# An explicit order for the first loads, and six planner numbers, in a packed-attention and ELU feed-forward kernel

## The chip, the core and the metric

The kernel runs on one core of a Trainium2 chip. The metric is the device time of one launch in microseconds. The core's engines are named as in the profile: PE (TensorE, matrix products; PEld is its weight load), DVE (VectorE), ACT (ScalarE), POOL (GpSimd) and SP (SyncE, which only issues the DMAs that are looked at here).

## What is computed

```python
def sm_attn(qq, kk, vv):                      # softmax attention, scale 1/sqrt(64)
    s = scale * np.matmul(qq, kk.transpose(0, 1, 3, 2))
    a = softmax(s)
    return np.matmul(a, vv)
p_packed = sm_attn(p, k, v)                   # p: (8, 8, 32, 64); q, k, v: (8, 8, 576, 64)
out      = sm_attn(q, p_packed, p_packed)
x = out.transpose(0, 2, 1, 3).reshape(4608, 512)
h = x @ w_in                                  # (512, 2048)
g = np.where(h > 0, h, np.exp(np.minimum(h, 0)) - 1)
result = g @ w_out                            # (2048, 512)
```

The attention inputs are 32-bit floats. The two weight matrices are given as 64-bit floats.

## The kernel before

**Work and tiles.** There are eight batches (b0 to b7) of 576 tokens. For each batch the kernel does the packed attention: scores of the 32 packed rows against the keys (`s1`, L476), softmax, transposes (`tr1`, L531), product with the values (`pv`, L557), a transpose (L583), then scores of the queries (`s2`, L602, in two halves) and their softmax, which ends in an "unfold" (a DVE transpose, L652) that gives the attention weights `a`. Instead of forming the attention output, it forms M = p_packed times w_in in four column pieces (`mstep`, L705), and h = a times M for sixteen feature blocks f of 128 (`mm`, L815 or L822, called the h steps here). ELU runs on ACT (L829, L835) and DVE (L838), and the output product (`out_mm`, L932 to L941) accumulates over f in PSUM.

**Weights.** Each of the 16 blocks of w_in (named i0 to i15 here) and of w_out (o0 to o15) arrives as a 512 KB tile `raw` of 64-bit words. Seven instructions turn it into 32-bit values: exponent (DVE, L280), sign (ACT, L292), power (ACT, L287), mantissa (DVE, L295), whole (DVE, L301), signed (DVE, L308) and product (DVE, L318). `whole` is the last reader of the raw tile. There are three raw buffers (L237), so a fourth raw load waits until the first tile has been read. For products that use split operands a value is cut in a high part (ACT, L252) and a low part (DVE, L331). The first four w_out blocks are used whole at first and are split later, with due times `T_WS + f` (L351, L352). The weights `a` of batches 0 and 1 are likewise used whole at first, and split at their first use plus `T_AS` (L679).

**The planner.** Every step of the kernel is an entry of a list with a due time, the engines that it may run on with a cost each, the entries that it depends on, and the buffers that it takes. `schedule` (L155) walks through planned time: whenever an engine is free, it takes the entry of earliest due time that is ready and has its buffers, and never interrupts a step. The instructions are then issued in that order, and each engine and the SP queue work strictly through their own list. The due times are counted in h steps: h step number i is due at i, its output product at i + `LOOK`. The conversion of a weight block is due `LI` or `LO` ahead of its first use, and an M piece of batches 0 and 1 `LM` ahead of it. The attention of b0 is due at -40 to -36, and its second `s2` half at `T_S2`. Batch 1 follows `T_ATT1`. Later batches follow `T_ATT` and `TM`.

**Modes of PE.** Entries on PE carry a mode: 1 for products with 64-row operands (s1, s2, mstep), 2 for pv, none for the rest. When the next entry would change the mode, the planner looks for a ready entry of the present mode whose due time is less than `STAY` later than that entry's (L183), and takes it instead.

**The first loads.** The loads of i0 to i3 are due at -60 to -57 and those of o0 and o1 at about -44 (L335). The loads of b0 are due at -46 (packed rows p and keys k), -45 (values v, in two parts) and -43 (queries q). All of these go through SP's one queue.

Of the kernel before, what the change touches and what calls it, by code (L numbers as in the profile page):

```python
# [20 lines left out]
def packed_attention_elu_ffn(  # L21
# [54 lines left out]


    T_ATT, T_ATT1 = [12, 14.0, 15.0, 16.0, 17.5, 17.5], [-12, -11, -11, -10, -10, -9]
    LI, LO, LM, LOOK = 4.5, 3.0, 2.5, 3.5
    TM = [24.5, 24.5, 28.0, 28.0]  # L80
    T_S2, STAY, SWITCH = 0, 4, 0.12

    F_PLAIN, H_PLAIN = 4, [0, 1]
    T_WS, T_AS = 20, 6

# [55 lines left out]
    def op(prio, on, fn, deps=(), take=(), use=(), after=(), mode=None):  # L145
        o = Op()
        o.prio, o.on, o.fn, o.deps = prio, on, fn, [d for d in deps if d is not None]
        o.after = [d for d in after if d is not None]
        o.take, o.end, o.n, o.mode = list(take), None, len(ops), mode
        for b in list(take) + list(use):  # L150
            b.users.append(o)
        ops.append(o)
        return o

    def schedule():  # L155
# [81 lines left out]
        raw=3, ex=2, sg=1, mi=2, p=2, ppT=3, pp=1, k0=1, q0=1,  # L237
# [10 lines left out]
    def ring_tile(ring, pool, shape, dt, tag, **kw):  # L248
        return Buf(R[ring], lambda: pool.tile(shape, dt, tag=tag, name=tag, **kw))
# [12 lines left out]
    def weights(f, first, prio):  # L262

        raw = ring_tile("raw", stg, [P, WC, 2], U32, "raw", bufs=3)
# [67 lines left out]
                out=wo(f, 1), in0=word(), in1=wo(f, 0).bitcast(F32), op=ALU.subtract  # L332
            )

        ld = op(-60 + f if first and f < 4 else -44 + f / 9 if f < 2 else prio - 8, {"DMA": 1.45}, load, take=[raw])  # L335
        x = op(prio, {"DVE": 0.42}, exponent, [ld], take=[ex_b], use=[raw])
        s = op(prio, {"ACT": 0.66}, sign, [ld], take=[sg_b], use=[raw])
        p = op(prio, {"ACT": 0.72}, power, [x], use=[ex_b])
# [4 lines left out]
        take = words_b if f % 2 == 0 else []  # L343
# [25 lines left out]
    def attention(b, ts):  # L369
# [86 lines left out]
        for name, fn, bufs, t in (  # L456
            ("k", load_k, k_b, ts[0] - 6), ("v", load_v, v_b, ts[0] - 5), ("q", load_q, q_b, ts[0] - 3),
        ):
            lds[name] = []
            for n, x in enumerate(bufs):  # L460
                prev_ld = op(
                    t, {"DMA": 3.3 / len(bufs)}, lambda e, fn=fn, n=n: fn(e, n),
                    take=[x] + ([p_b] if (name, n) == ("k", 0) else []), after=[prev_ld],
                )
                lds[name].append(prev_ld)
# [17 lines left out]
        def smax1(e, g):  # L483
            if g == 0:
                sv["mx"] = small.tile([P, G], F32, tag="mx", name="mx")
            nc.vector.tensor_reduce(  # L486
                out=sv["mx"][:, g:g + 1], in_=ps1[g].t[:, :, :HS], axis=AX.XY, op=ALU.max
            )

        def neg(e, g):  # L490
            if g == 0:
                sv["nb"] = small.tile([P, G], F32, tag="nb", name="nb")
                sv["sm"] = small.tile([P, G], F32, tag="sm", name="sm")
            nc.vector.tensor_scalar(
                out=sv["nb"][:, g:g + 1], in0=sv["mx"][:, g:g + 1], scalar1=-SCALE, scalar2=None,
                op0=ALU.mult,
            )
# [8 lines left out]
        def srec1(e):  # L506
# [6 lines left out]
        o1 = op(ts[0], {"PE": 1.0}, s1, ld_k, take=ps1 + e1s, use=[p_b] + k_b,  # L513
                after=[prev_b.tmp_last if b > 1 else None], mode=1)
        o4s, o = [], None
        for g in range(G):
            o = op(ts[0], {"DVE": 0.76}, lambda e, g=g: smax1(e, g), [o1], use=[ps1[g]], after=[o])
            o = op(ts[0], {"DVE": 0.16}, lambda e, g=g: neg(e, g), [o])
# [4 lines left out]
        for g in range(G):  # L523
# [19 lines left out]
            t = ts[1]  # L543
# [20 lines left out]
        o = op(ts[2], {"PE": 0.85}, pv, ld_v + tr_done, take=[ps, pp_b], use=v_b + e1T, mode=2)  # L564
# [25 lines left out]
        o = op(ts[3], {"PE": 0.06}, tr2, done, take=[pt2, st.ppT], use=[pp_b])  # L590
# [3 lines left out]
        for half in range(2):  # L594
# [62 lines left out]
            def lo(e, cs=cs, done=done):  # L657
# [5 lines left out]
            t = ts[4 + half]  # L663
            o = op(t, {"PE": 0.52}, s2, [lds["q"][half % len(q_b)], st.ppT_op],
                   take=[ps, t1], use=[q_b[half % len(q_b)], st.ppT], mode=1)
            f0 = op(t, {"DVE": 0.44}, lambda e, fold=fold: fold(e, 0), [o] + prev, use=[ps, t1])
            f1 = op(t, {"DVE": 0.44}, lambda e, fold=fold: fold(e, 1), [f0], use=[ps, t1])
            o = op(t, {"DVE": 0.75}, smax, [f1], use=[t1])
            o = op(t, {"DVE": 0.76}, ssub, [o], use=[t1])
            o = op(t, {"ACT": 0.69}, sexp, [o], use=[t1])  # L670
            o = op(t, {"DVE": 0.75}, ssum, [o], use=[t1])
            o = op(t, {"DVE": 0.43}, srec, [o])
            o = op(t, {"DVE": 0.75}, smul, [o], use=[t1])
            take = [] if whole and half else [t2]
            o = op(t, {"DVE": 0.77}, unfold, [o], take=take, use=[t1] + ([] if take else [t2]))
            prev = [o]
            st.af_done.append(o)
            if whole:
                t = first_use["b", b] + T_AS  # L679
            h = op(  # L680
                t, {"ACT": 0.67, "DVE": 0.4}, hi, [o] + st.a_done[-1:],
                take=[st.a] if half == 0 else [], use=[t2] + ([st.a] if half else []),
# [86 lines left out]
    for b in range(B):  # L769
        if b == 0:  # L770
            ts = [-40 + n for n in range(5)] + [T_S2]
        elif b < NB0:
            ts = [first_use["b", b] + t for t in T_ATT1]
        else:
            ts = [first_use["b", b] - NS + t for t in T_ATT]
        sts[b] = attention(b, ts)
# [4 lines left out]
    for f in range(NF):  # L781
        weights(f, True, first_use["f", f - f % 2] - LI)
        weights(f, False, first_use["f", f] - LO)
# [12 lines left out]
    for i, (b, win, f) in enumerate(order):  # L796
        st = sts[b]
        c, o = divmod(f * P, FC)
# [95 lines left out]
        if odd_half:  # L894
# [13 lines left out]
            take=into["take"] if g_whole else [], after=into["after"] if g_whole else [],  # L908
# [13 lines left out]
        first = i == 0 or visit_of[i - 1] != v_n  # L922
# [5 lines left out]
        def out_mm(e, f=f, g_b=g_b, acc=acc, first=first, final=final, g_whole=g_whole):  # L928
# [17 lines left out]
            take=acc if first else [], use=[g_b] + ([] if first else acc),  # L946
# [68 lines left out]
```

## Time and profile before

| | |
|---|---|
| median of 3 runs | 725.22 us (725.15 to 725.24) |
| profiled execution | 724.5 us, with a span of 722.3 us in the trace |
| PE busy | 699.6 us (97% of the span) |
| DVE busy | 504.4 us (70%) |
| ACT busy | 387.4 us (54%) |
| DMA | 61.42 MB, mean 85 GB/s |

The 2.2 us between the span and the profiled execution's time lie outside of the trace. The profile's busy time of PE is modelled from pipelined matmuls, so a busy PE need not be at its peak. Idle time of an engine that is not the bottleneck costs nothing by itself.

### The profile page before, as it was taken

The page shows a single profiled execution, that of the slowest core. Times are in us where ns is not written, and L with a number is a line of the kernel's source. Part 1 is how long each engine was busy: PE and PEld are TensorE (multiplying, and loading weights), DVE is VectorE, ACT ScalarE, POOL GpSimd, SP SyncE. Part 2 cuts the span into 40 slices and gives each one's busy share as a digit, 9 for nine tenths or more (in the row PEclk, how much of TensorE's full clock was granted, in tenths as well). Part 3 has the DMA queues.
Part 4 walks back from the last instruction along what each step waited for, and adds up shares of the span by engine and source line. Part 5 has one row for each costly group of instructions (what it writes and reads, how often), then busy time and mean ns, then how long its engine had stood idle before and what let it go on. Part 6 is the DMA issues. An engine that isn't in the chain of part 4 may idle for free.

```text
span 722.3 us, 13401 instructions
## 1 busy us (share of the span) xinstructions
PE 699.6 (97%) x5076; PEld 557.1 (77%) x5076; DVE 504.4 (70%) x1256; ACT 387.4 (54%) x900; POOL 19.4 (3%) x27
## 2 busy tenths in 40 slices
PE   2799999999999999999999999999999999999997
PEld 1454588887778877888878887888888877888886
DVE  6999998886875587545875569555686559654453
ACT  5777888885654455434454445434454345444332
POOL 0000002110111000000000000000000000000000
PEclk9999999999999999999999999999999999999999
DMA  9846546634543430003300250001400040000010
GB/s 348 296 150 204 186 147 142 132 66 108 165 59 44 123 108 1 30 1 128 117 2 29 67 165 1 2 29 66 160 21 1 30 132 30 1 30 1 0 45 30
DMA packets 29360, 61.42 MB, mean 85 GB/s; under 512 B 2544, under 2 KB 11760, under 8 KB 29040
## 3 DMA queue, kind: packets, MB, share of 16 engines
q1 hardware_dynamic: 26272, 55.06, 22.6%
q0 software_dynamic: 3024, 5.51, 5.6%
q8 instruction: 40, 0.66, 0.4%
q14 instruction: 24, 0.20, 0.1%
HBM read 45.61 MB, written 14.94 MB: 84 GB/s over the span
## 4 chain that ended last, share of the span: by engine, by line
PE 96%; DVE 1%; DMA 1%; ACT 1%; issue 0%; SPq 0%; ACTq 0%
PE psum L822 27%; PE psum L938 18%; PE psum L939 17%; PE psum L941 17%; PE psum L932 4%; PE psum L705 4%; PE psum L815 2%; PE psum L557 2%; PE psum L531 1%; PE psum L476 1%; PE psum L602 1%; DMA k<-in_kT 1%; DVE mx L486 0%; ACT tmp L500 0%; SPq L275 0%
## 5 line engine op out<-in xcount | busy, mean ns | idle before, releaser
L829 ACT ACTIVATE e<-psum 128x256 f32<-128x256 f32 (+1 forms) x256 | 105.4, 412 | 236.2 <-PE psum L822 214.4
L838 DVE SCALAR_TENSOR_TENSOR e<-e,psum 128x256 f32<-128x256 f32 (+1 forms) x240 | 103.6, 432 | 106.8 <-ACT e L835 106.1
L822 PE MATMUL psum<-a_hi,m_hi 128*128 128x256 f32 (+1 forms) x480 | 146.5, 305 | 0.0
L822 PE MATMUL psum<-a_lo,m_hi 128*128 128x256 f32 (+1 forms) x480 | 142.0, 296 | 0.0
L822 PE MATMUL psum<-a_hi,m_lo 128*128 128x256 f32 (+1 forms) x480 | 141.9, 296 | 0.0
L861 DVE TENSOR_TENSOR g_lo<-e,g_hi 128x256 fp32r<-128x256 f32 (+1 forms) x240 | 105.3, 439 | 22.0 <-ACT g_hi L252 7.1
L835 ACT ACTIVATE e<-e 128x256 f32<-128x256 f32 (+1 forms) x256 | 114.0, 445 | 6.1
L938 PE MATMUL psum<-wo_b,g_hi 128*128 128x512 f32 x288 | 114.8, 398 | 0.0
L939 PE MATMUL psum<-wo_b,g_hi 128*128 128x512 f32 x288 | 113.6, 394 | 0.0
L822 PEld LDWEIGHTS psum<-a_hi,m_hi 128*128 128x128 f32 x480 | 90.5, 189 | 24.2 <-issue 9.6
L938 PE MATMUL psum<-wo_a,g_hi 128*128 128x512 f32 x252 | 99.4, 394 | 0.0
L939 PE MATMUL psum<-wo_a,g_hi 128*128 128x512 f32 x252 | 99.3, 394 | 0.0
L822 PEld LDWEIGHTS psum<-a_lo,m_hi 128*128 128x128 f32 x480 | 90.7, 189 | 8.7 <-issue 1.0
L822 PEld LDWEIGHTS psum<-a_hi,m_lo 128*128 128x128 f32 x480 | 90.6, 189 | 0.0
L941 PE MATMUL psum<-wo_b,g_lo 128*128 128x512 f32 x288 | 86.6, 391 | 0.0
L941 PE MATMUL psum<-wo_a,g_lo 128*128 128x512 f32 x252 | 76.1, 392 | 0.0
L938 PEld LDWEIGHTS psum<-wo_b,g_hi 128*128 128x128 f32 x288 | 54.2, 188 | 12.1 <-issue 3.6
L941 PEld LDWEIGHTS psum<-wo_b,g_lo 128*128 128x128 f32 x288 | 54.1, 188 | 12.1
L252 DVE CAST g_hi<-e 128x256 fp32r<-128x256 f32 (+1 forms) x180 | 54.0, 300 | 12.5 <-PE psum L939 3.7
L939 PEld LDWEIGHTS psum<-wo_b,g_hi 128*128 128x128 f32 x288 | 54.3, 189 | 7.6
L941 PEld LDWEIGHTS psum<-wo_a,g_lo 128*128 128x128 f32 x252 | 47.3, 188 | 10.5
L938 PEld LDWEIGHTS psum<-wo_a,g_hi 128*128 128x128 f32 x252 | 47.5, 188 | 9.4 <-ACT g_hi L252 2.5
(88 smaller groups left out, 761.3 us busy)
## 6 DMA issues: line engine op xcount, KB each, us to landing
out<-part SPq DMA_DIRECT2D x36, 256.0 KB, 2.2
raw<-in_w_in SPq DMA_DIRECT2D x16, 512.0 KB, 3.7
kvq<-in_v SPq DMA_DIRECT2D x16, 512.0 KB, 5.1
raw<-in_w_out SPq DMA_DIRECT2D x16, 512.0 KB, 3.5
kvq<-in_kT SPq DMA_DIRECT2D x14, 576.0 KB, 4.5
kvq<-in_qT SPq DMA_DIRECT2D x14, 576.0 KB, 4.6
out<-part POOLq DMA_DIRECT2D x21, 256.0 KB, 4.4
k<-in_kT SPq DMA_DIRECT2D x1, 1152.0 KB, 7.4
```

What stands on the lines that cost most here:

```text
L252: (nc.scalar.copy if e == "ACT" else nc.vector.tensor_copy)(out=out, in_=in_)
L557: nc.tensor.matmul(ps.t[cols_of(pair), g, :D], lhsT=e1T[g].t[:n, c, cols_of(pair)], rhs=values(c, h)[:n], start=(c == 0), stop=(c == NKC - 1),
L705: nc.tensor.matmul(ps.t[cols_of(pair), g, :w], lhsT=st.ppT.t[rows_of(g), pair, :], rhs=w_in_sb[rows_of(g), pair, c * FC + part * w:c * FC ...
L822: nc.tensor.matmul(ps_b.t[:, :n_tok], lhsT=m_b[x].t[:, g, o:o + P], rhs=st.a.t[y][:, g, cols], start=(n == 0), stop=(n == 3 * G - 1),)
L829: nc.scalar.activation(out=e_b.t[:, :n_tok], in_=ps_b.t[:, :n_tok], func=AF.Relu, scale=-1.0)
L835: nc.scalar.activation(out=x, in_=x, func=AF.Exp, scale=-1.0)
L838: nc.vector.scalar_tensor_tensor(out=out, in0=e_b.t[:, cs], scalar=-1.0, in1=ps_b.t[:, cs], op0=ALU.add, op1=ALU.max)
L861: nc.vector.tensor_tensor(out=g_b.t[1][:, cs], in0=x, in1=g_b.t[0][:, cs].bitcast(F32), op=ALU.subtract)
L932: nc.tensor.matmul(a.t, lhsT=g_b.t[0][:, t].bitcast(F32), rhs=w_words[f // 2].t[:, f % 2, :], start=first, stop=final,)
L938: nc.tensor.matmul(a.t, lhsT=g_b.t[0][:, t], rhs=wo(f, 0), start=first, stop=False)
L939: nc.tensor.matmul(a.t, lhsT=g_b.t[0][:, t], rhs=wo(f, 1), start=False, stop=False)
L941: nc.tensor.matmul(a.t, lhsT=g_b.t[1][:, t], rhs=wo(f, 0), start=False, stop=final)
```

## The change

The first nine loads are given an explicit order: i0, i3, o0, i2, i1, k (with p), v, o1, q, due at -60 to -52 in that order. Six numbers are said to be set anew; in the diff the planner numbers that differ are `LM` (2.5 to 1.5), `STAY` (4 to 3), `T_WS` (20 to 23) and `T_AS` (6 to 8). No instruction is added or removed, and no buffer count and no planner cost is changed.

```diff
-    LI, LO, LM, LOOK = 4.5, 3.0, 2.5, 3.5
+    LI, LO, LM, LOOK = 4.5, 3.0, 1.5, 3.5
     TM = [24.5, 24.5, 28.0, 28.0]
-    T_S2, STAY, SWITCH = 0, 4, 0.12
+
+    FIRST = "i0 i3 o0 i2 i1 k v o1 q".split()
+    T_S2, STAY, SWITCH = 0, 3, 0.12
 ...
-    T_WS, T_AS = 20, 6
+    T_WS, T_AS = 23, 8
 ...
-        ld = op(-60 + f if first and f < 4 else -44 + f / 9 if f < 2 else prio - 8, {"DMA": 1.45}, load, take=[raw])
+        name = ("i" if first else "o") + str(f)
+        t = FIRST.index(name) - 60 if name in FIRST else prio - 8
+        ld = op(t, {"DMA": 1.45}, load, take=[raw])
 ...
             lds[name] = []
+            if b == 0:
+                t = FIRST.index(name) - 60
             for n, x in enumerate(bufs):
```

## Rows read from the trace of the kernel before

**Rows 1.** The page: busy time of PE, its share of the span, instructions.

```profile
PE 699.6 (97%) x5076; PEld 557.1 (77%) x5076; DVE 504.4 (70%) x1256; ACT 387.4 (54%) x900; POOL 19.4 (3%) x27
```

**Rows 2.** Stretches of 20 us: busy time by engine, granted clock, DMA share, GB/s.

```profile
0.00:20.00 20.00, 6.97 (x122) 4.77 (x122) 14.39 (x35) 11.56 (x21) 0.70 (x6) 1.00 0.93 353
20.00:40.00 20.00, 14.87 (x221) 9.17 (x211) 18.20 (x42) 14.91 (x35) 0.00 (x0) 0.91 0.80 275
40.00:60.00 20.00, 20.00 (x126) 9.04 (x125) 19.43 (x46) 13.38 (x27) 0.00 (x0) 1.00 0.52 177
```

**Rows 3.** PE's waits: total us, times, longest us.

```profile
PE psum L476 <- DMA k<-in_kT: 10.1, 1, 10.1
```

**Rows 4.** Timeline of SP's DMA issues, start us and us, up to 12 us.

```profile
0.74 1.34 SPq L275 DMA_DIRECT2D raw<-in_w_in  x3
...
2.59 0.64 SPq L429 DMA_DIRECT2D k<-in_kT  x1
6.12 0.33 SPq L275 DMA_DIRECT2D raw<-in_w_in  x1
...
8.20 0.48 SPq L442 DMA_DIRECT2D kvq<-in_v  x1
8.79 2.07 SPq L275 DMA_DIRECT2D raw<-in_w_out  x2
```

**Rows 5.** Single DMA issues of rows 4: KB, and us from issue to landing.

```profile
k<-in_kT SPq DMA_DIRECT2D x1, 1152.0 KB, 7.4
...
raw<-in_w_in SPq DMA_DIRECT2D x1, 512.0 KB, 5.2
...
kvq<-in_v SPq DMA_DIRECT2D x1, 64.0 KB, 6.6
...
raw<-in_w_out SPq DMA_DIRECT2D x1, 512.0 KB, 7.2
```

**Rows 6.** Timeline of PE: start us, us, line, count, idle time before and releaser.

```profile
10.15 2.18 PE L476 MATMUL psum<-k,p 64*32 64x288 f32 x32 [10.15 <-DMA k<-in_kT]
...
17.41 2.77 PE L557 MATMUL psum<-kvq,tmp 128*32 128x64 f32 x80
...
29.35 0.77 PE L531 MATMUL psum<-ident,tmp 128*128 128x128 f32 x5 [2.46 <-ACT tmp L500]
...
31.85 2.78 PE L815 MATMUL psum<-k,m_hi 128*128 128x256 f32 x8
34.56 1.46 PE L557 MATMUL psum<-kvq,tmp 128*32 128x64 f32 x80
```

**Rows 7.** Timeline of ACT between b0's transposes and its product with the values.

```profile
16.24 0.74 ACT L252 COPY tmp<-psum 128x512 f32<-128x512 f32 x2 [0.55 <-PE psum L531]
17.30 0.59 ACT L252 COPY tmp<-psum 128x512 f32<-128x512 f32 x1 [0.33 <-PE psum L531]
17.79 0.68 ACT L292 ACTIVATE sg<-raw 128x512 bf16<-128x512 f32 x1
18.36 0.26 ACT L252 COPY tmp<-psum 64x128 f32<-64x128 f32 x1
```

**Rows 8.** Timeline of DVE: conversion work beside b0's softmax.

```profile
21.20 0.43 DVE L308 TENSOR_TENSOR ex<-ex,sg 128x512 bf16<-128x512 bf16 x1 [0.73 <-ACT sg L292]
...
29.60 0.15 DVE L494 TENSOR_SCALAR nb<-mx 128x1 f32<-128x1 f32 x1
29.67 0.68 DVE L318 SCALAR_TENSOR_TENSOR w_words<-mi,ex 128x512 f32<-128x512 f32 x1
30.27 0.77 DVE L652 STREAM_TRANSPOSE k<-tmp 128x576 f32<-128x576 f32 x1
```

**Rows 9.** Stretches of 2 us, columns as in rows 2.

```profile
30.00:32.00 2.00, 1.39 (x8) 1.24 (x7) 1.97 (x7) 1.97 (x6) 0.00 (x0) 0.55 0.97 355
32.00:34.00 2.00, 2.00 (x7) 1.61 (x6) 2.00 (x5) 1.49 (x4) 0.00 (x0) 0.59 0.13 46
```

**Rows 10.** Chain that ended last, start us and us, around the s2 halves of b3 and b4.

```profile
252.77 0.65 PE psum L602 x16
253.41 0.43 PE psum L938
253.84 0.23 PE psum L939
...
344.75 1.13 PE psum L602 x32
```

**Rows 11.** Low parts of b1's a (tile q), and PE's first split h step.

```profile
L658 DVE TENSOR_TENSOR a_lo<-q,a_hi x2: 747/751/755, 61.8 to 68.2; 128x576 fp32r<-128x576 f32 x2
...
81.26 0.68 PE L822 MATMUL psum<-a_hi,m_hi 128*128 128x256 f32 x1
```

## The prediction

> **What bounds the kernel now.** I read the page first. PE is busy 97% of the span [rows 1], so I ask where the missing 22.7 us (722.3 - 699.6) are. The table by stretches of 20 us answers: 13.0 us of them lie in the first 20 us and 5.1 us in the next 20; from 40 to 60 us PE is full [rows 2], and only 4.6 us are left for all the rest, the tail included. An order of loads and due times removes no PE work. It can change three things: those 18.1 us, the clock in that stage, and the number of times that PE changes between kinds of products. Next come PE's waits: 10.1 us of the 18.1 are one wait, for b0's keys [rows 3]. The remaining 8 us lie in gaps between b0's and b1's attention steps, the longest in sight being the 2.46 us before b1's transposes [rows 6]. In this stage the granted clock is 0.55 and 0.59 of full from 30 to 34 us [rows 9], that is nearly all of the time at the lower of its two levels, 1.2 GHz where the other is 2.4. The work lost there is 2 x 0.45 + 2 x 0.41 = 1.7 us.
>
> What sets the end of the gaps? The first h step (L815) starts at 31.85 us [rows 6], and it needs b0's unfolded weights, which DVE has at 30.27 + 0.77 = 31.04 us [rows 8]. DVE is busy nearly throughout by then, with b0's softmax and conversions side by side. So DVE's order is what counts from 22 us on, and ahead of that the chain keys, s1, transposes, pv.
>
> **Part 1: the order of the first loads.** Listed sixth, the keys still leave fourth. Three raw buffers are filled by i0, i3 and o0. In the planner's costs the third load ends at 3 x 1.45 = 4.35, while i0's last reader (`whole`) ends at 5.35 at the earliest (landing at 1.45 + 2.2 = 3.65, then mantissa and whole at the planner's costs). At 4.35 i2 and i1 find no buffer, and k, which has its own, is taken. Before, k also stood behind three raw tiles of 512 KB [rows 4], and landed at 2.59 + 7.4 = 10.0 us [rows 5]. The bytes ahead are the same, so the 10.1 us wait stays: 0 us. What would cost something is in the rivals.
>
> Walked on by hand, the planner's rules give after k: i2, the first half of v, i1, the second half of v, o1, q. Before it was i3, v, v, o0, o1, q [rows 4]. On SP, i1 now waits for i3's `whole`, and behind it in that queue stand half of v, o1 and q. I work out about 9.9 us for that issue. By then i2 and half of v are still on the way (the load that landed fourth before did so at 6.12 + 5.2 = 11.3 us [rows 5]), so the DMA engines have work and the wait is hidden. The price if that cover is gone is the gap itself, under 1 us on v. The whole of v came at 8.20 + 6.6 = 14.8 us before [rows 5]; with one more raw tile ahead (512 KB at 353 GB/s [rows 2], 1.5 us) it comes at 16.3 us, and pv starts at 17.41 us [rows 6]. So v costs 0, with 1.1 us of cover. The set of bytes ahead of q is unchanged.
>
> The conversions: between the s1 products and 22 us DVE used to have i3 (landed 11.3 us), o0 (8.79 + 7.2 = 16.0 us [rows 5]) and o1. Now it has i2, i1 and o1. i1 follows i2 with half of v between, 1.1 MB at 353 GB/s, 3.1 us, so it lands near 14.4 us. The number of instructions is the same, but i1 is there 1.6 us earlier than o0 was. The one DVE hole there, 0.73 us behind a sign of o1 on ACT [rows 8], should close. I count half of it as reaching the softmax: -0.4 us (bounds 0 and -0.7).
>
> The other side: on ACT, i1's sign and power are now ready between b0's transpose copies. Before, the copies ran at 16.24 us (two) and 17.30 us, and o0's sign came only after the third [rows 7]. In the planned order, i1's sign (0.68 us, the row of o0's) stands behind the first copy. The third copy then ends at 16.24 + about 0.5 + 0.6 + 0.2 + 0.59 = 18.1 us instead of 17.9 us, and pv with it: +0.25 us (bounds 0 and +0.7, a whole sign on the path).
>
> Then the stretch from the first fold to the unfold. The walk gives the same steps with the same fillers, but for the last: before, a small DVE step of 0.15 us and o2's product of 0.68 us came right ahead of the unfold [rows 8], where b1's second maximum had gone earlier. Now that maximum takes the place, and these two fall behind the unfold: -(0.15 + 0.68) plus about 0.1 for overlap, -0.7 us. In exchange b1's second transpose group, which stood ahead of the first h step, comes behind it. It is work that has to be done either way.
>
> Sum of part 1: -0.4 + 0.25 - 0.7, about -0.9 us at the first h step.
>
> **Part 2: the due times.** `LM` moves the M pieces of b0 and b1 one h step later, and `STAY` lets a change of mode come one step earlier: these nearly cancel, 0 us. `T_AS` makes b1's split weights due at h step 16, their very first use. Before, the last low part started at 68.2 us and the first split h step at 81.26 us [rows 11], 12 us of cover. Even if two steps of the list moved it by as much as lies between b1's two low parts, 6.4 us, it would be early: 0 us. `T_WS` moves the splits of four w_out words from due times of 20 to 23 to 23 to 26. They are fillers without a reader nearby: 0 us, and at most the 0.69 us (the planner's cost) of one such step.
>
> `STAY` also acts on b2 to b7. The rows show what a split group costs. Two s2 halves together take 1.13 us, alone 0.65 us each, and the first product after each return to the 128-row products takes 0.43 us instead of 0.23 us [rows 10]: 2 x 0.65 - 1.13 + 0.20 = 0.37 us for each group that falls apart. In the chain b3, b5 and b7 have their s2 halves apart, as b3 in these rows, and their M pieces in three groups; b4 and b6 have the halves together, as b4, and two groups of M. If the three became like the two, six groups would merge, -2.2 us; the other way four would fall apart, +1.5 us. These are the bounds. Which groups change depends on which PSUM banks are free when the step comes up, which I cannot follow that far. I take 0, between the ends, because nearly all groups are bound by banks and not by due times.
>
> Sum: 725.22 - 0.9 = 724.3 us as a median. The profiled execution's own 724.5 us, 0.7 us under the median, would become 723.6 us, with a span of 721.4 us.
>
> **The rivals.**
>
> *Faster: the low clock stretch goes away.* If the gaps from 24 to 31 us shrink, PE may keep its full clock and get back the 1.7 us: 724.3 - 1.7 = 722.6 us; with all six groups merged 720.4 us, and with a further gap closed a little less. For it: the gaps are what came before the fall. Against: the walk still leaves b1's s1 and its first transposes where they were.
> The Trainium skill ("TensorE: Matmul & The Clock Gate", Part 1) says that the throttled state is the default and that activity releases it. The trace agrees in that the fall follows the emptiest PE stretch after the keys came; by this rule, fuller gaps would give this rival and emptier ones the next.
>
> *Slower: a new hole behind the first h steps.* Before, b1's pv (1.46 us at 34.56 us [rows 6]) filled the time in which the third h step waited for the ELU of the first. With b1's second transposes later, pv is no longer ready there. The hole would be up to that 1.46 us, and if it keeps the clock low for a second stretch like the first, 1.7 us more: 724.3 + 1.4 + 1.7 = 727.4 us. It decides from the point where b1's pv becomes ready later than the third h step does.
>
> *Slower: the keys really go sixth.* If i2 and i1 found buffers in time, 1.05 MB more would precede k: 1.05 MB / 353 GB/s [rows 2] = 3.0 us on PE's longest wait, 727.3 us. The buffer count speaks against it.
>
> **How the numbers follow.** Forecast (small gain, 723.8 to 726.6 us): 0.42. Faster by the clock or by merged groups: 0.38. New hole: 0.15. Keys sixth: 0.05. The measurement can tell about 0.2% from no change, 1.45 us, so the limits are 723.8 and 726.7 us. The forecast lies inside them, with a small part over the lower one (0.02). Faster 0.40, same 0.40, slower 0.20. The range: below, the merged groups and the clock together, with a little for a further gap, 719.8 us; above, the two slower cases, 727.5 us.
>
> **What would show it.** In the profile after: the wait of PE for k at 10.1 us again (13 us would mean that the keys went sixth); SP's issues in the order i0, i3, o0, p, k, i2; b0's unfold ending near 30.1 us and the first h step ahead of b1's second transposes; the granted clock from 30 to 34 us; the counts of the s2 and M groups (x16 or x32) in the chain; PE full from 40 us on. The prediction is wrong if PE's gaps up to 40 us change by more than 2 us, or if the groups of the later batches change, which I left at 0.

## The result and the profile after

| | before | after |
|---|---|---|
| median of runs | 725.18 us (724.03 to 725.62) | 728.23 us (727.68 to 729.83) |
| profiled execution, span | 724.5 us, 722.3 us | 727.68 us, 725.5 us |

The ratio is 1.0043, 95% interval 1.0026 to 1.006: the change makes the kernel about 0.4% slower. Measured twice more (after_again and after_third below), it gave 1.0038 (1.0023 to 1.0052) and 1.0034 (1.0019 to 1.005). The forecast was 724.3 us, with a range of 719.8 to 727.5 us. One of the two repeats, 727.12 us, lies inside that range, but a gain of 0.9 us was forecast and all three measurements show a loss of 2 to 3 us. Single executions of one kernel differ by as much: of 141 executions of the kernel before, the 71 with a mean granted clock of 0.997 or 0.998 took 724.8 us in the mean and the 25 with 0.991 or 0.992 took 727.4 us, so medians are compared here.

The page of after answers [rows 1]: PE is busy longer, for the same 5076 products.

```profile
PE 702.0 (97%) x5076; PEld 558.1 (77%) x5076; DVE 503.6 (69%) x1252; ACT 387.8 (53%) x904; POOL 19.5 (3%) x27
```

Stretches of after, columns as in [rows 2]:

```profile
0.00:20.00 20.00, 6.95 (x122) 4.74 (x122) 14.10 (x35) 12.04 (x23) 0.69 (x6) 1.00 0.91 346
20.00:40.00 20.00, 15.49 (x217) 9.24 (x210) 17.63 (x39) 14.53 (x35) 0.00 (x0) 0.91 0.78 264
40.00:60.00 20.00, 19.49 (x122) 8.64 (x122) 18.34 (x44) 11.35 (x25) 0.00 (x0) 1.00 0.45 154
...
180.00:200.00 20.00, 19.04 (x221) 14.06 (x220) 12.77 (x32) 12.09 (x29) 1.75 (x2) 1.00 0.58 153
```

Two things differ from [rows 2]. DVE has done 1.95 us less by 60 us (14.39 + 18.20 + 19.43 before, 14.10 + 17.63 + 18.34 now). And PE, full from 40 to 60 us before, misses 0.51 us there, and 0.96 us from 180 to 200 us (0.06 us before).

Where the 3.2 us of span went is read from equal work: I give each product of PE the duration of its shape at full clock, add them up in both traces, and compare the times at which the sums are equal. The difference, called the lag of after here, is -0.1 us at 17.5 us, +1.8 from 65 to 165 us, +1.4 at 190 us, and a constant +3.0 from 205 us to the end. The rows agree: b3's s1 starts at 240.04 us (237.05 before), b7's s1 at 581.19 us (578.14), so 3.0 us are lost ahead of b3 and nearly nothing behind it. There are two losses: 1.8 us before 65 us, and 1.2 us more in the stretch of b2's attention, where the lag jumps behind 190 us.

**The keys and the queue.** SP's first issues of after, answering [rows 4], and PE's waits, answering [rows 3]:

```profile
0.74 0.86 SPq L277 DMA_DIRECT2D raw<-in_w_in  x2
1.65 0.42 SPq L277 DMA_DIRECT2D raw<-in_w_out  x1
...
2.59 0.71 SPq L433 DMA_DIRECT2D k<-in_kT  x1
```

```profile
PE psum L482 <- DMA k<-in_kT: 10.0, 1, 10.0
PE psum L537 <- ACT tmp L506: 5.3, 2, 2.8
...
PE psum L608 <- DMA kvq<-in_qT: 1.5, 2, 1.0
```

The keys leave at 2.59 us as before and PE waits 10.0 us for them: being listed sixth changed nothing for them.

**The first loss.** PE's timeline of after, answering [rows 6]:

```profile
21.89 1.21 PE L608 MATMUL psum<-q,ppT 64*32 64x288 f32 x16 [0.35 <-ACT ppT L254]
...
25.56 2.78 PE L482 MATMUL psum<-kvq,p 64*32 64x288 f32 x32
30.86 2.40 PE L537 MATMUL psum<-ident,tmp 128*128 128x128 f32 x10 [2.52 <-ACT tmp L506]
33.05 2.48 PE L821 MATMUL psum<-k,m_hi 128*128 128x256 f32 x8
...
37.76 0.33 PE L589 MATMUL psum<-ident,pp 128*128 128x128 f32 x1 [0.83 <-ACT pp L575]
...
42.69 0.72 PE L608 MATMUL psum<-kvq,ppT 64*32 64x288 f32 x16 [0.51 <-DMA kvq<-in_qT]
```

Here b1's two transpose groups both stand ahead of the first h step, as they did before, and two waits of 0.83 and 0.51 us stand behind it, for b1's own later steps. The s2 half at 21.89 us took 1.21 us and b1's s1 2.78 us, against 0.72 and 1.67 us before: this stretch ran mostly at the lower level, 1.2 GHz. The clock records of the two traces put the rise to the full level at 27.3 us here and at 20.0 us before. DVE's timeline, answering [rows 8]:

```profile
28.40 0.76 DVE L492 TENSOR_REDUCE mx<-psum 128x1 f32<-128x576 f32 x1 [1.12 <-PE psum L482]
29.08 0.74 DVE L636 TENSOR_REDUCE sm<-tmp 128x18 f32<-128x576 f32 x1
...
30.86 0.42 DVE L282 TENSOR_SCALAR ex<-raw 128x512 uint16<-128x512 uint16 x1
31.19 0.75 DVE L645 TENSOR_TENSOR tmp<-tmp,sm 128x576 f32<-128x576 f32 x1
31.86 0.42 DVE L297 TENSOR_SCALAR mi<-raw 128x512 uint32<-128x512 uint32 x1
32.19 0.77 DVE L658 STREAM_TRANSPOSE k<-tmp 128x576 f32<-128x576 f32 x1
```

b1's first maximum now stands ahead of the sum of b0's softmax, and waits 1.12 us for b1's s1; the unfold, at 30.27 us before, starts at 32.19 us. In a second profile of after, in which the clock rose at 19.7 us (after_again below), that wait is 0.55 us and the unfold starts at 30.67 us.

**The second loss.** The chain of after near 190 us. The step of 7.83 us is the load of the second half of b2's queries (before, the two halves took 4.6 us from issue to landing and were not in the chain).

```profile
185.24 0.78 PE psum L828 x4
186.01 7.83 DMA kvq<-in_qT
193.84 0.14 issue
193.98 0.72 PE psum L608 x16
```

b2's s1 runs at 173.84 us (168.75 before), its pv at 183.78 us (179.14), and the load, whose buffer pv gives back, is issued at 185.26 us (180.63). In after two accumulating stores of POOL are issued 0.72 us ahead of it, at 184.54 us; before, they followed it by 4.1 us, at 184.74 us. The issues of both loads and stores, first after, then before, with size and median time from issue to landing of the loads:

```profile
184.54 1.75 POOL L970 DMA_DIRECT2D out<-part  x2 [14.36 <-ACT part L254]
185.26 1.32 SPq L454 DMA_DIRECT2D kvq<-in_qT  x2
kvq<-in_qT SPq DMA_DIRECT2D x2, 576.0 KB, 6.6
```

```profile
180.63 1.32 SPq L450 DMA_DIRECT2D kvq<-in_qT  x2
184.74 1.75 POOL L964 DMA_DIRECT2D out<-part  x2 [15.82 <-ACT part L252]
kvq<-in_qT SPq DMA_DIRECT2D x2, 576.0 KB, 4.6
```

### The profile page after: what moved, and what is told of

The parts are those of the page before. It is cut to its first block, busy times and chain, and to the rows that moved or that the text cites. A ratio compares the mean times of both kernels' runs of the same rounds, so it can differ in the third digit from the quotient of the medians.

```text
span 725.5 us, 13408 instructions
## 1 busy us (share of the span) xinstructions
PE 702.0 (97%) x5076; PEld 558.1 (77%) x5076; DVE 503.6 (69%) x1252; ACT 387.8 (53%) x904; POOL 19.5 (3%) x27
## 2 busy tenths in 40 slices
DMA packets 29360, 61.42 MB, mean 85 GB/s; under 512 B 2544, under 2 KB 11760, under 8 KB 29040
## 3 DMA queue, kind: packets, MB, share of 16 engines
q1 hardware_dynamic: 26272, 55.06, 22.5%
## 4 chain that ended last, share of the span: by engine, by line
PE 93%; DMA 4%; DVE 1%; ACT 1%; SPq 0%; issue 0%; DVEq 0%; ACTq 0%
PE psum L828 27%; PE psum L944 18%; PE psum L945 17%; PE psum L947 17%; PE psum L938 4%; PE psum L711 4%; DMA raw<-in_w_out 2%; PE psum L821 2%; DMA kvq<-in_qT 2%; PE psum L563 1%; PE psum L537 1%; PE psum L608 1%; PE psum L482 1%; DMA raw<-in_w_in 1%; ACT sg L294 0%; DVE ex L282 0%
```

## The experiments

Three causes were on the table: the order of the work in the engines' lists at the start (the holes above); the moment at which the clock rises; and the load of b2's queries that meets the stores (theory C in the expectations). The diffs are cut to the lines that matter, with values on one line where the code has several. Lags are those of the profiled executions against the first profile of before, as explained above. The kernel before was measured again beside each group of runs: 725.17 to 725.58 us.

**Either half of the change alone.** The order with the old numbers, the numbers with the old order, and after with only `T_AS` set back:

```diff
 order_only: after with
+    LM = 2.5; STAY = 4; T_WS, T_AS = 20, 6
 numbers_only: before with
+    LM = 1.5; STAY = 3; T_WS, T_AS = 23, 8
 after_as6: after with
+    T_AS = 6
```

> The explicit load order alone, with the four numbers of before (2.5, 4, 20, 6). In the two traces the changed kernel has lost 1.8 us by 65 us and 3.05 us by 205 us, and nothing after. Theory A (the load order makes the start late: the sign of i1 between the transpose copies, pv and s2 later, PE's clock rising only at 27.3 us instead of 20.0 us): the products at 22 us take 1.2 us per 16 s2 instructions as in the changed kernel (0.72 us before), b0's unfold comes near 32.2 us again, and the start costs 1.5 to 2.2 us. What the second loss does here is not said by theory A; in this kernel's list b2's s1 stands early (near 60 us of PE work), so that b2's queries should be loaded long before their use: 726.2 to 727.4 us in all. Rival B (the numbers cost it all): the start is as before, 725.2 us within 0.5.

Measured: 734.29 us, 1.0117 (1.0096 to 1.0138), which neither theory had. Its first 35 us have the lists of after, with the clock as in the first profile of before: up at 19.9 us, at the lower level from 30.2 to 33.6 us. Its lag at 65 us is 1.0 us even so; the load order costs that much at the start without the four numbers and without a late clock. Most of its loss lies elsewhere: b2's s1 runs at 88.07 us, and the following attention work of b2 falls into a stage in which DVE has no room. Stretches of order_only, and a row of its PE timeline:

```profile
112.00:116.00 4.00, 2.46 (x28) 1.72 (x28) 3.74 (x9) 3.90 (x9) 0.48 (x1) 1.00 0.95 208
116.00:120.00 4.00, 1.54 (x29) 0.79 (x37) 4.00 (x9) 4.00 (x9) 0.00 (x0) 0.87 0.68 161
120.00:124.00 4.00, 3.56 (x24) 2.10 (x25) 4.00 (x10) 3.48 (x8) 0.00 (x0) 0.50 0.39 134
```

```profile
119.89 1.11 PE L711 MATMUL psum<-w_in_sb,ppT 64*32 64x256 f32 x16 [1.94 <-DVE m_lo L724]
```

The lag is +0.6 us at 110 us and +9.3 at 120 us: PE waits for DVE's low parts of M, and the clock falls to its lower level after these emptier 8 us.

> The four numbers alone, with the first loads of before. Theory A: the list up to 40 us is nearly that of before, so the unfold ends near 31.0 us and the clock rises near 20 us; the start costs less than 0.5 us. b2's s1 stands as late in the list as in the changed kernel, so the wait of b2's second s2 half for its queries near 190 us should be there with about 1 us: 725.2 to 726.6 us. Rival B: 727.5 to 728.5 us.

Measured: 726.55 us, 1.0018 (1.0003 to 1.0034): b2's s1 at 173.01 us, nearly as late as in after, but its load of q is issued at 183.63 us, ahead of the stores (186.86 us), and no wait for it follows. The clock rose at 24.9 us in the profile and was at the lower level again from 28.3 to 35.1 us, so its lag of 1.8 us at 65 us doesn't tell the numbers from the clock.

> The changed kernel with T_AS at 6 again. The list is the same up to about 60 us, and b2's s1 moves from 141 us to 109 us of PE work, so that its values and queries are loaded some 30 us earlier. Theory A plus C (the second loss is the wait for b2's queries, and T_AS is what made their load late): the start stays late by 1.8 us, and the 1.2 to 1.5 us near 190 us are gone: 726.6 to 727.2 us. Rival D (that wait has its cause in LM or in the late start): it stays, 728.2 us.

Measured: 737.65 us, 1.0166 (1.0143 to 1.0188). The lag goes from +2.6 us at 120 to +12.6 at 200. So setting `T_AS` back does not repair after, and the time is far above both expectations (726.6 to 728.2 us). b2's s1 comes at 141.55 us, 32 us sooner. The loss is not quite that of order_only. From 155 to 175 us DVE is busy for 14.0 of 20 us, so it isn't full; PE waits for both halves of b2's queries and then for a low part of M, and the clock is at its lower level from 163.6 to 170.4 us. Rows of its PE timeline:

```profile
163.89 1.22 PE L608 MATMUL psum<-kvq,ppT 64*32 64x288 f32 x16 [1.46 <-DMA kvq<-in_qT]
166.35 1.21 PE L608 MATMUL psum<-kvq,ppT 64*32 64x288 f32 x16 [1.25 <-DMA kvq<-in_qT]
172.59 0.50 PE L944 MATMUL psum<-wo_b,g_hi 128*128 128x512 f32 x1 [2.46 <-DVE m_lo L724]
```

The parts don't add: +1.2% and +0.2% make +0.4%. By the plans that `schedule` makes, both `T_AS` and `LM` of after are needed to keep b2's attention late, and with the order of before it stays late with either setting; only `T_AS` was set back alone in a run.

**The clock.** Products with an identity matrix, whose results nobody reads, keep PE busy before the keys come and between the first groups (48, 24 and 16 of them, then 24 and 8).

```diff
+        for _ in range(24):
+            nc.tensor.matmul(out=psum[:, 0, :P], lhsT=ident, rhs=ident, start=True, stop=True)
```

> The kernel before with added products of the identity on PE whose results are overwritten: 48 ahead of everything, 24 ahead of b0's transposes and 16 ahead of b1's. They keep PE busy while it would wait. Theory A (PE's clock in the first 35 us is worth time): s1 takes 1.1 to 1.3 us instead of 2.18, pv 1.4 to 1.6 instead of 2.77, the clock does not fall at 30 us, and the time falls by 2 to 4 us: 721.5 to 723.2 us. Rival (DVE alone sets the start, the clock is hidden): within 0.7 us of 725.2.

> The changed kernel with the same added products. Theory A (most of the start's loss is the later rise of PE's clock): with the clock up in both, the start's difference to the kernel before shrinks from 1.8 us to under 0.8 us, and only the wait for b2's queries stays, 1.2 to 1.5 us: 1.3 to 2.3 us slower than the kernel before with the same products. Rival E (the order of the fillers on DVE and ACT costs the start, whatever the clock): 2.8 to 3.5 us slower than that kernel.

> The changed kernel with T_AS at 6 and the same added products. Theory A plus C: neither the start's loss nor the wait for b2's queries is left, so it is within 0.8 us of the kernel before with the same products. Rival E: 1.5 to 2 us slower than that one.

Measured: 737.46, 741.8 and 748.88 us, ratios 1.0179, 1.0225 and 1.0338. The added products were mis-sized: in before_warm the three groups took 12.45, 7.25 and 5.47 us themselves and stood in the way. after_warm is 4.3 us slower than before_warm and after_as6_warm 11.4 us, both more than any of the theories had. With fewer:

> The kernel before with fewer added products of the identity, none of which has to wait for the softmax: 24 ahead of the keys and 8 right behind b0's s1. The first such trial spent 12.4 us and 7.3 us on them and was slower by its own products. Theory A (the low clock up to 20 us is worth time): s1 takes 1.1 to 1.3 us, pv 1.4 us, and the first h step starts 1 to 2.5 us earlier: 722.7 to 724.3 us. Rival (DVE sets the start): within 0.7 us of 725.2 us.

> The changed kernel with the same 24 and 8 added products. In the profiles taken so far PE's clock rose for good only at 20 us in some (the kernel before, order alone, T_AS at 6) and at 25 to 27 us in others (the changed kernel, the numbers alone), with the same instructions ahead of it. Theory G (the clock's rise is a matter of the single run and no part of the change): with the products in both, the distance to the kernel before stays 2.5 to 3.3 us. Theory A (the late rise belongs to the change): the distance falls to 1.3 to 2.3 us.

Measured: 727.44 us, 1.0025 (1.001 to 1.0039) and 729.86 us, 1.006 (1.004 to 1.008). In before_warm2 b0's s1 took 1.21 us (2.18 before) and the lag was -2.1 us at 17.5 us, but the added products took 8.47 and 2.05 us of PE themselves, and PE then waited for ACT instead. Its timeline:

```profile
20.09 0.33 PE L589 MATMUL psum<-ident,pp 128*128 128x128 f32 x1 [1.80 <-ACT pp L575]
21.23 1.22 PE L608 MATMUL psum<-q,ppT 64*32 64x288 f32 x16 [0.81 <-ACT ppT L252]
```

The clock fell again from 21.0 to 24.4 us, and the lag was +1.0 from 45 us on. In this trial, then, an early clock bought nothing that lasted, and the distance between before and after stayed: 2.4 us here, 1.8 to 3.2 us in the three comparisons without the products.

**The same kernels again.**

> The kernel before, a second time, for another profile and more times. Theory G (the moment at which PE's clock rises differs between runs of the same list): the time is 725.2 us within 0.7, and the profile may show the rise at another place than 20.0 us, with the s2 products of b0 at 1.2 us per 16 instructions if it is later. Theory A: the rise stays within 0.3 us of 20.0 us.

> The changed kernel a second time. Theory G: 728.2 us within 0.8; the profile's clock may rise near 20 us this time, and then PE's lag against the kernel before at 65 us is 1.0 to 1.4 us instead of 1.8, with the second loss near 190 us as it was (1.2 to 1.6 us). Theory A: the clock rises after 24 us again, and the lag at 65 us is 1.7 to 1.9 us.

Measured: 725.31 and 727.12 us, ratio of the latter 1.0038. This pair separates the clock from the lists, since in both profiles it rose at 19.7 us. The spans are 722.1 and 724.9 us; b1's s1 in after_again took 2.44 us, its first h step started at 32.21 us (31.93 in before_again), and the lag was +0.1 at 22.5 us, +1.0 at 65, +0.6 at 190 and +2.4 from 200 us on (before_again: -0.1 at 65, -0.25 from 200 on). So with the clock alike 2.8 us of the 3.2 us of span remain: 1.1 at the start and 1.6 in the stretch of b2's attention. One pair of profiles carries this split. The late clock of the first profile of after was worth the difference of the two spans of after, 0.6 us. In other executions more is lost ahead of the second loss, with a longer stretch at the lower level: b2's s1 runs at 173.00, 173.84 and 175.94 us in three profiles of after (after_again, the first, and after_third below, whose clock rose at 27.4 us and was at the lower level from 30.8 to 37.6 us). And where before's own list had the lower level from 26.9 to 37.1 us (before_touch below), it runs at 171.60 us, against 168.62 and 168.75 us.

**The holes at the start.** b1's transpose and s2 moved back by hand in the finished plan, behind the h step and the output product that follow them:

```diff
+        move(sts[1].tr2_op, h_ops[2], 1)
+        move(out_ops[1], sts[1].s2_ops[0], 0)
```

> The changed kernel with two entries of PE's list moved as they stood before: the third h step ahead of b1's last transpose, and the second output product ahead of b1's s2. In the changed kernel PE stands idle 0.83 us ahead of that transpose and 0.51 us in b1's s2, waiting for its queries. Theory F (the order of PE's list at 35 to 43 us costs the start 1 to 1.4 us): the two idle times fall under 0.3 us in sum, PE's lag at 50 us falls by 0.8 to 1.3 us, and the time is 726.9 to 727.5 us. Rival (DVE sets the pace there, and what is gained is waited for at the next h step): the lag at 65 us is as in the changed kernel, within 0.3 us, and the time 728.2 us.

Measured: 728.06 us, 1.0031 (1.0013 to 1.0049). The two waits are gone, and one for b0's second unfold on DVE stands in their place:

```profile
44.52 2.42 PE L824 MATMUL psum<-k,m_hi 128*128 128x320 f32 x8 [0.81 <-DVE k L659]
```

The lag at 65 us is 1.3 us. But the profile doesn't settle whether PE's order was the cause: the clock was at the lower level from 28.7 to 35.5 us here, twice as long as in after_again (30.0 to 33.4 us), and the first eight h products took 3.75 us (2.47 us there). The median, 0.2 us under that of after, shows no gain within its interval.

**The keys truly first, or third.**

```diff
-    FIRST = "i0 i3 o0 i2 i1 k v o1 q".split()
+    FIRST = "k i0 i1 i2 v i3 o0 o1 q".split()     (keys_first)
+    FIRST = "i0 i1 k i2 v i3 o0 o1 q".split()     (keys_third)
```

> The changed kernel with another order of the first loads: k i0 i1 i2 v i3 o0 o1 q. In the planned queue p and k stand first, then three raw tiles, v, i3, q. Theory H (PE's wait for the keys is worth its length): k lands near 6 us, s1 starts there, and the first h step comes 2 to 4 us earlier than in the changed kernel: 724.5 to 726 us. Rival (DVE's conversions set the first h step, and they now start 3 us later): the first h step comes within 1 us of 33.05 us, and the time is 727.5 to 729 us.

> The changed kernel with the first loads in the order i0 i1 k i2 v i3 o0 o1 q: k behind two raw tiles instead of three. Theory H: k lands near 8.7 us, 1.3 us earlier, and the first h step comes 0.7 to 1.5 us earlier: 726.5 to 727.7 us. Rival: within 0.5 us of 728.2 us.

Measured: 734.84 us, 1.0137 (1.0116 to 1.0157), and 731.55 us, 1.0096 (1.008 to 1.0113). PE's waits of keys_first:

```profile
PE psum L482 <- DMA k<-in_kT: 6.6, 1, 6.6
...
PE psum L482 <- ACT tmp L632: 2.5, 1, 2.5
...
PE psum L821 <- DVE nb L500: 1.5, 1, 1.5
```

In keys_first the keys came 3.4 us sooner than in after and the first h step 3.2 us sooner than in before (28.69 us, against 31.85 us). But the lag, -3.6 us at 17.5 us, was +2.1 at 36 and +7.9 at 40 us, with new waits for ACT, DVE and b1's queries, while the clock was at its lower level from 22.2 to 32.4 and from 39.3 to 49.5 us. In keys_third the keys came only 0.5 us sooner, at 9.58 us. In these two orders PE's longest wait was therefore no price that could be taken off the end. They also move the other loads and the attention of later batches, so what bounds the start in their place isn't told apart.

**The load of b2's queries.** First without the two accumulating stores (512 KB of 61.42 MB; the part of the result that they add is left out), then with all the work, but with the stores behind a POOL read of one column of the loaded queries:

```diff
+                    if v_n == 9:      # after_nostore9
+                        return
```

```diff
+        plan[n:n] = moved             # after_store_late: both stores behind b2's last load of q
+                touch = small.tile([P, 1], F32, tag="touch", name="touch")
+                nc.gpsimd.tensor_copy(out=touch, in_=sts[2].q_b[1].t[:, :1])
```

> The changed kernel without the two accumulating stores of b1's second window, features 8 to 15 (256 KB each, issued by POOL at 184.5 us); this part of the result is left out. In the changed kernel they are issued just ahead of b2's query load (185.3 us), whose second half takes 7.8 us to land where it took 4.6 us before, and PE's lag against the kernel before grows from 1.4 to 2.9 us there. Theory C (the second loss is this load, late by b2's place in the list and slowed by the two stores): the second half lands in under 6 us, PE's wait for it goes or falls under 0.3 us, and the kernel takes 0.8 to 1.5 us less than the changed one: 726.7 to 727.5 us. Rival (the load is simply issued too late): the wait stays, within 0.4 us of 728.2 us.

> The kernel after, with nothing left out: the two accumulating stores that were issued at 184.54 us now stand behind a one-column read by POOL of b2's second half of q, so they go only when that load has landed; every engine's list is otherwise that of after. Theory C (the two stores slow the load of q, 7.8 us from issue to landing against 4.6 us before): the load lands about 3 us sooner, PE's wait for q at 194 us (0.96 us) goes, and the distance from the h steps of 185 us to those of 205 us that after lost (1.5 to 1.9 us) goes with it: 0.2% less than after_third, about 726.3 us. Rival (what helped when the stores were left out was the missing traffic and work, not the collision, or the load is late by itself, being issued 4.6 us later): the wait stays at 0.5 us or more and the time is that of after_third within 0.1%, about 727.7 us.

> The kernel after, unchanged, on the same chip as the run beside it. Between 727.1 and 728.2 us by the two earlier measurements, a ratio of 1.003 to 1.005 to the kernel before, with PE's wait for q near 194 us.

Measured: after_nostore9 726.3 us, 1.0011 (0.9996 to 1.0025); after_store_late 725.92 us, 1.0006 (0.9992 to 1.002); after_third 728.47 us, 1.0034 (1.0019 to 1.005). POOL's timeline and PE's wait of after_store_late:

```profile
191.60 0.19 POOL L991 COPY touch<-kvq 128x1 f32<-128x1 f32 x1 [21.01 <-DMA kvq<-in_qT]
191.83 1.76 POOL L972 DMA_DIRECT2D out<-part  x2
```

```profile
PE psum L609 <- DMA kvq<-in_qT: 0.5, 1, 0.5
```

The halves of q land in a median 4.7 us (4.6 without the stores, 6.3 to 6.9 in the three profiles of after). From b2's s1 to b3's s1, the same list in each, it takes 66.20, 66.47 and 66.01 us in the three profiles of after, 65.16 us without the stores and 65.02 us with late stores. So the meeting of load and stores costs 0.9 to 1.4 us in these profiles. The remaining wait of 0.5 us is the one for b1's queries, at 43 us.

**A gain that was not asked for.** In after_store_late another 0.9 us went between b3's s1 and b7's s1: 340.26 us, against 341.1 to 341.2 us elsewhere. The added read alone, in after and in before:

> The kernel after, its stores where they were, with the one-column read of b2's second half of q by POOL added behind that load (and behind the two stores). The run with late stores took back some 1.2 us between b2's s1 and b3's s1 and, unexplained, another 0.9 us between b3's s1 and b7's s1 (340.26 us against 341.15 us). If the late stores alone bring the first part, the distance from b2's s1 to b3's s1 is again 66.0 us or more here, with PE's wait for q near 194 us. If the added tile or instruction brings the second part (all later tiles lie elsewhere in SBUF), b3's s1 to b7's s1 takes 340.2 to 340.3 us and the time is 0.9 us under after's, about 727.0 us; if not, 341.1 to 341.2 us and about 727.9 us.

> The kernel before with the same added read of one column behind b2's load of q. If the added tile or instruction speeds up the later batches, b3's s1 to b7's s1 takes 340.2 us instead of 341.1 us and the time is 0.9 us under before's, about 724.4 us, ratio 0.9988; if not, 725.3 us, ratio 1.000.

Measured: after_touch 727.34 us, 1.0014 (1.0 to 1.0029); before_touch 724.41 us, 0.9983 (0.997 to 0.9997). b3's and b7's s1 in before_touch:

```profile
239.76 1.20 PE L477 MATMUL psum<-kvq,p 64*32 64x288 f32 x32
579.98 1.20 PE L477 MATMUL psum<-kvq,p 64*32 64x288 f32 x32
```

The distance is 340.22 us, in after_touch 340.26 us. So the gain of 0.9 us belongs to the added tile or its instruction and not to the stores. In after_touch the stores are where they were, and PE waits for q again, with the halves landing in a median 8.2 us:

```profile
194.43 0.72 PE L609 MATMUL psum<-kvq,ppT 64*32 64x288 f32 x16 [1.91 <-DMA kvq<-in_qT]
```

From b2's s1 to b3's s1 this profile takes 68.56 us, 3.5 us more than after_store_late with the same added read: behind the wait the clock was at its lower level from 195.9 to 199.3 us, which none of the other profiles of after has. It is the slowest of 12 executions (729.97 us), so it shows how far the cost can go and not the usual one. Of the 2.55 us between after_store_late and after_third some 0.9 us are the touch, and 1.65 us are left for the late stores; against after_touch the ratios leave them 0.08%, 0.6 us. The 0.9 to 1.4 us from the rows lie between; the intervals of after_touch and after_store_late overlap, so the size is known only roughly. before_touch is the fastest kernel of this study, 1.17 us under the kernel before on the same chip.

## Why the prediction was wrong, step by step

- **What bounds the kernel: half right.** The first 40 us and the groups were looked at; the stretch near 190 us, full in before, was not suspected. PE full from 40 us on was named as a sign, and it fails in both places. The other sign, PE's gaps up to 40 us, misled: they shrank by 0.6 us (13.03 + 5.13 before, 13.05 + 4.51 after), because the same products took longer at the lower clock. And the longest gap behind the keys is 2.79 us at 15.11 us, ahead of b0's transposes, not the 2.46 us ahead of b1's; nothing rests on that.
- **Keys fourth, 0 us: right**, with the three raw buffers as the reason. The queue's order came out as worked out, with i1 issued at 9.81 us (9.9 forecast) and its cover in place: pv starts at 17.30 us [rows 6: 17.41], so v cost nothing.
- **i1's sign on ACT, +0.25 us: right in kind.** ACT's timeline, answering [rows 7], has it behind the first copy, and pv ends at 17.96 + 2.31 = 20.27 us against 20.18 us: +0.1 us.

```profile
16.13 0.59 ACT L254 COPY tmp<-psum 128x512 f32<-128x512 f32 x1 [0.55 <-PE psum L537]
16.61 0.67 ACT L294 ACTIVATE sg<-raw 128x512 bf16<-128x512 f32 x1
17.17 0.74 ACT L254 COPY tmp<-psum 64x128 f32<-64x128 f32 x2
```

- **DVE's hole closes, -0.4 us: wrong.** In the first profile of after two other holes opened, 0.62 us (18.87 us) and 0.66 us (22.89 us), both for w_out tiles that had not landed yet. In after_again neither is there, and the first fold still starts at 22.31 us (22.27 us before), right behind the end of s2 at 21.43 + 0.72 = 22.15 us: the hole was not on the path to the softmax.
- **Nothing but b1's maximum ahead of the unfold, -0.7 us: wrong, and the step that failed first.** The maximum stands ahead of the sum and waits there, and two instructions of a conversion (0.42 us each, `ex` and `mi`) stand ahead of the unfold. With the clock alike the first h step came 0.3 us later, not 0.9 us sooner. The walk by hand had only b1's second maximum there.
- **New hole behind the first h steps (0.15): the nearest of the rivals in place.** Its own mechanism didn't come: b1's second transposes stand ahead of the h step, and pv fills its place (35.47 us). The holes, 0.83 and 0.51 us, are one and two steps on, and the clock did not fall again. With DVE's delay the start lost 1.1 us, where the rival had 3.1 us above the forecast.
- **The clock:** the stretch at the lower level from 30 to 34 us is there in both [rows 9]; the rise was late in the first profile of after (27.3 us), in after_store_late and after_third too, but not in after_again (19.7 us). It moves from one execution to the next with the list unchanged, and so does the length of the lower stretch. The prediction had no term for that; between profiles of one list, of after as of before, b2's s1 moves by up to some 3 us with it.
- **`LM`, `T_AS` and `T_WS` at 0 us: wrong for `LM` and `T_AS`.** Their own readers were covered, as argued: the last low part of b1 starts at 75.4 us and takes 0.75 us, and the first split h step starts at 82.30 us [rows 11], some 6 us of cover. But an entry that moves gives its place to another. Which one was not asked: b2's attention. That is worth +1.2 to +1.6 us in after, most of it by the load of q that meets the stores, and in order_only, where it goes the other way, some 7.4 us (b3's s1 runs at 245.41 us, 8.4 us later than before, of which 1.0 us is the start). In the plans, `T_WS` alone changes no engine's list.
- **`STAY` at 0 us: right for the batches that were priced.** The chain of after, answering [rows 10], has b3's s2 halves apart and b4's together, as before. b3's M pieces are still in three groups; only which two are joined changed. b2's groups, which the prediction didn't list, did change: its s2 halves and two pieces of M ran as one group at 184.98 us before and as three in after (188.62, 191.23 and 193.98 us). With the wait for q gone (after_nostore9) the h steps fall behind by only 0.1 us more across that stretch, so this is the small part of the second loss.

```profile
255.78 0.65 PE psum L608 x16
...
347.78 1.13 PE psum L608 x32
...
267.93 1.02 PE psum L711 x16
273.69 1.02 PE psum L711 x16
283.95 1.88 PE psum L711 x32
```

In sum the failed steps are the -0.4 and -0.7 us of part 1, which with the rest of part 1 (-0.9 us) became +1.1 us, and the 0 us of `LM` and `T_AS`, which became +1.6 us (sizes from the pair with the clock alike). With these two terms the sum is 725.2 + 1.1 + 1.6 = 727.9 us; the three medians of after are 727.12, 728.23 and 728.47 us.

What stays open: which place in the lists of PE or DVE costs the 1.1 us at the start (order_only ties it to the load order; moving PE's steps gave no gain in the median, but under a longer lower stretch in its profile, and DVE's list was not moved alone), and what in the added tile or read speeds up the later batches.

## What to carry to other kernels

In a list-scheduled kernel with in-order queues a change of a due time is costed by what takes the freed place, not by the readers of the entry that moves: compare the whole lists, and follow the first entries of the next batch, their buffers and the transfers that these release. A transfer's cover depends on what else is in flight when it is issued; look for stores within a few microseconds of each load that a busy engine needs. And the longest wait is no price by itself: here the keys could come 3.4 us sooner and the kernel was 1.4% slower. Before a loss of a few tenths of a per cent is explained from two profiles, take each kernel's profile more than once: the start alone moved by some 3 us here with the list unchanged.

## What the runs showed of the hardware

- Two 576 KB loads that took a median 4.6 us from issue to landing took 6.3 to 6.9 us, and 8.2 us in after_touch, when two accumulating 256 KB stores were issued 0.7 us ahead of them.
- The rise of PE's granted clock at the start came between 18.5 and 27.6 us in executions whose lists are alike or nearly so up to then. The same 32 products (b1's s1) took 1.67 us in before, at the full level, and 2.78 us in after, mostly at the lower one. The stretch at the lower level that followed lasted from 3.4 us (before, after) to 10.2 us (before_touch).
- One more tile of 4 bytes per partition, with a read of one column, made the same lists from b3's s1 to b7's s1 0.9 us shorter (340.2 us against 341.1 us), in three kernels of three. That the later tiles lie elsewhere in memory may explain it, but no run shows it.
